# A 7-tap convolution and a two-layer channel mixer in fp32 on one core: the third group's second matmul is taken as seven half products, with the weight sums and several transfers moved

## The chip, the cores and the metric

One core of a Trainium2 chip. The metric is the device time of one execution in microseconds; lower is better. All data is fp32.

## What is computed

```python
# x: (8, 4224, 192); weight: (8 heads, 7 taps); w1: (192, 768); w2: (768, 192)
w = softmax(weight, axis=-1)
y[b, s, h*24 + g] = sum_k w[h, k] * x[b, s - 6 + k, h*24 + g]     # zeros ahead of s = 0
xn = (y - mean(y)) / sqrt(var(y) + 1e-6) * g_ln                   # over the 192 channels
out = y + relu(xn @ w1) @ w2
```

## The kernel before, in words

**Groups.** The rows are cut into NG = 18 groups of 128 partitions by n rows: n is 6, 8 (the rows left over, from all eight sequences), 10, and then 16 for the other fifteen. Group g is one turn of the loop at L973. `groups` (L70) holds them. Group 0, 1 and 2 are the start of the pipeline.

**What a group needs.** `load_x` (L132) brings x with six rows of padding into a tile `xg` (two buffers in turn, so a load waits until the group two before it is done with its x). The convolution is split by taps: tap 0 by `first_tap` on ScalarE (ACT; L369), tap 1 for some groups by `second_tap` (L382), which makes the product on ACT into a tile `tb` and adds it to y by an accumulating DMA on GpSimd's (POOL's) queue, the other taps by `conv` on VectorE (DVE; L397), one instruction for each tap and head (24 channels). `transpose` (L408) makes yt, in 32 by 32 blocks, six chunks of 32 channels. `moments` and `root` (L425, L436) make 1/sqrt(var), which is applied only at the end; the mean is taken out of w1 beforehand.

**The two matmuls.** On TensorE (PE) each fp32 matmul stands in the trace as two records. Groups 0 to 2 do them plainly: `up` (L525) runs six hidden tiles f, each over six chunks c and four blocks q, and `evict_up` (L495) takes each tile out of PSUM with a ReLU on ACT into `ht`, a view of the big tile `room`; `down` (L738) runs six output chunks over six f and four q. From the fourth group on (`fast[g]` not zero; L76, `MIXED` L81), both are Winograd products: matrices in quarters, seven half-size products where the plain form has eight. `up_mixed` (L587) and `down_fast` (L789) do that. They need sums of quarters of w1 and w2 (`w1sums`, `w2sums`, by `sums_of_quarters`, L555), of yt (`sums_of_y`, L569) and of the hidden values (`half_sum`, `lower_sum`, L770 and L777). In `down_fast` the order is: product 1 (a11), product 2 (a21 after `lower_sum`), products 3 and 4; then DVE's `transpose` of the next group, three half sums in place, which may overwrite a12, a11 and a22 only once PE has read them; products 5, 6 and 7 read those. `finish` or `finish_fast` turn the results back into rows; `scale` (ACT) applies the factor and `add_to_out` adds to the output in DRAM by an accumulating DMA on POOL's queue, onto y, which `store_y` (L472) has put there.

**What sets the order.** The whole kernel is in a manual schedule: each engine, and each DMA queue, executes its instructions in the order of the program text, and waits only for data. So the text of the loop L973 to L1027 is the order. In turn g = 0: up(0), conv(1) in two halves of heads with a transpose after each (chunks 0 to 2, then 3 to 5), store of y1, moments, first_tap(2), down(0). In g = 1: conv(2) with six taps, transpose(2), store of y2, first_tap(3), down(1), finish(0), the sums of w2 on DVE, finish(1). In g = 2: conv(3) with six taps, transpose(3), first and second tap of group 4, store of y3 on POOL, down(2), the four sums of w1 on DVE (the last one in place in w1), sums_of_y(3) wholly on DVE, finish(2), moments(3). At its end each of these three groups is parked by ACT copies from PSUM (`park`, L863). Each `load_x(g + 2)` stands at the head of turn g, on SyncE's (SP's) queue. The weights are joined from two words each just before: w1 is complete with the last copy of L360, w2 with L246, L249 and L255 on DVE (`join_words`), called after up(0)'s first tile.

## Time and profile before

| what | value |
|---|---|
| median of 3 runs | 960.58 us (960.49 to 960.9) |
| the profiled execution: its own time | 960.25 us |
| its span, first to last instruction | 958.5 us |
| PE busy | 948.6 us (99%) |
| DVE busy | 895.8 us (93%) |
| ACT busy | 686.6 us (72%) |
| POOL busy | 260.9 us (27%) |
| mean granted TensorE clock | 0.999 of full |
| DMA | 166.69 MB, mean 174 GB/s |

PE's matmuls are pipelined, so its busy share alone doesn't say that it is at its peak. A row of the groups or of the timeline reads: start and length (or busy time), engine, line of the kernel, operation, what it writes and reads, the shapes, how many; in square brackets the idle time of the engine just before and what ended it. A piece of the chain of waits reads: start, length, engine and line, number of instructions. L519 is the matmul of `up` and `up_mixed`, L753 that of `down`, L806 that of `down_fast`.

### The profile page before, as it was taken

The page shows a single profiled execution, that of the slowest core. Times are in us where ns is not written, and L with a number is a line of the kernel's source. Part 1 is how long each engine was busy: PE and PEld are TensorE (multiplying, and loading weights), DVE is VectorE, ACT ScalarE, POOL GpSimd, SP SyncE. Part 2 cuts the span into 40 slices and gives each one's busy share as a digit, 9 for nine tenths or more (in the row PEclk, how much of TensorE's full clock was granted, in tenths as well). Part 3 has the DMA queues.
Part 4 walks back from the last instruction along what each step waited for, and adds up shares of the span by engine and source line. Part 5 has one row for each costly group of instructions (what it writes and reads, how often), then busy time and mean ns, then how long its engine had stood idle before and what let it go on. Part 6 is the DMA issues. An engine that isn't in the chain of part 4 may idle for free.

```text
span 958.5 us, 38499 instructions
## 1 busy us (share of the span) xinstructions
PE 948.6 (99%) x17274; PEld 719.5 (75%) x17274; DVE 895.8 (93%) x1510; ACT 686.6 (72%) x1139; POOL 260.9 (27%) x399
## 2 busy tenths in 40 slices
PE   8999999999999999999999999999999999999997
PEld 7886596776869687786958678686867768586787
DVE  8999998999999999999999999999989999999667
ACT  6625578596877959687796958778695877866461
POOL 1005311612135131422216131341315221161400
PEclk9999999999999999999999999999999999999999
DMA  8243887679697887969788796978879697767241
GB/s 221 79 155 112 180 207 216 146 151 265 134 260 142 235 173 158 249 123 276 136 240 163 178 234 118 281 136 243 158 186 216 120 280 141 179 132 129 53 83 68
DMA packets 28394, 166.69 MB, mean 174 GB/s; under 512 B 3397, under 2 KB 4294, under 8 KB 22215
## 3 DMA queue, kind: packets, MB, share of 16 engines
q0 software_dynamic: 21568, 100.94, 55.0%
q1 hardware_dynamic: 6656, 63.31, 17.9%
q8 instruction: 135, 2.21, 0.9%
q14 instruction: 29, 0.24, 0.1%
q10 hardware_dynamic: 6, 0.00, 0.0%
HBM read 38.93 MB, written 50.33 MB: 93 GB/s over the span
## 4 chain that ended last, share of the span: by engine, by line
PE 97%; ACT 1%; DMA 1%; DVE 0%; SPq 0%; issue 0%; ACTq 0%
PE ps L519 48%; PE ps L806 42%; PE ps L753 6%; DMA xg<-in_x_dram 1%; PE ps L322 1%; ACT w L360 0%; ACT room L618 0%; DVE y L898 0%; ACT spare L241 0%; ACT y L378 0%; PE ps L335 0%; SPq L215 0%; ACT room L509 0%; PE ps L350 0%; SPq L210 0%
## 5 line engine op out<-in xcount | busy, mean ns | idle before, releaser
L403 DVE SCALAR_TENSOR_TENSOR y<-xg,taps,y 128x384 f32<-128x384 f32 (+3 forms) x734 | 367.9, 577 | 1.8 <-issue 1.6
L519 PE MATMUL ps<-yt,w 32*128 32x256 f32 (+2 forms) x4104 | 235.7, 379 | 0.4 <-ACT room L509 0.4
L806 PE MATMUL ps<-room,w2sums 128*32 128x256 f32 (+1 forms) x4320 | 235.9, 375 | 0.0
L618 ACT COPY room<-ps 128x1024 f32<-128x1024 f32 (+1 forms) x135 | 175.0, 1296 | 77.2 <-PE ps L519 76.0
L519 PEld LDWEIGHTS ps<-yt,w 32*128 32x128 f32 x4104 | 204.2, 185 | 26.5 <-issue 9.0
L806 PEld LDWEIGHTS ps<-room,w2sums 128*32 128x32 f32 x4320 | 140.5, 110 | 89.7 <-ACT room L631 4.9
L806 PE MATMUL ps<-room,w 128*32 128x256 f32 (+1 forms) x3240 | 181.0, 375 | 0.4 <-issue 0.4
L773 DVE TENSOR_TENSOR room<-room 128x1024 f32<-128x1024 f32 (+1 forms) x135 | 151.6, 1196 | 21.2 <-PE ps L806 20.0
L806 PEld LDWEIGHTS ps<-room,w 128*32 128x32 f32 x3240 | 104.8, 110 | 68.7 <-DVE room L624 5.0
L519 PE MATMUL ps<-ysums,w1sums 32*128 32x256 f32 x2160 | 124.9, 379 | 0.0
L519 PEld LDWEIGHTS ps<-ysums,w1sums 32*128 32x128 f32 x2160 | 108.7, 185 | 11.2 <-ACT room L618 3.6
L812 ACT COPY cs<-ps 128x256 f32<-128x256 f32 (+1 forms) x180 | 66.0, 369 | 42.6 <-PE ps L806 42.6
L884 ACT ACTIVATE ot<-ot,r 128x192 f32<-128x192 f32 x232 | 93.8, 462 | 0.0
L631 ACT ACTIVATE room<-room 128x1024 f32<-128x1024 f32 (+1 forms) x89 | 92.1, 1071 | 0.0
L891 POOL DMA_DIRECT2D out_dram<-ot x40 | 34.2, 1086 | 194.6 <-ACT ot L884 115.7
L378 ACT ACTIVATE y<-xg,taps 128x384 f32<-128x384 f32 (+3 forms) x141 | 72.8, 611 | 9.0 <-DVE st L434 7.6
L434 DVE BATCH_NORM_STATS2 st<-y 128x6 f32<-128x192 f32 x264 | 70.2, 344 | 0.0
L519 PE MATMUL ps<-yt,w1sums 32*128 32x256 f32 x1080 | 65.1, 379 | 0.0
L812 ACT COPY room<-ps 128x256 f32<-128x256 f32 (+1 forms) x90 | 33.6, 373 | 43.9 <-PE ps L806 42.4
L519 PE MATMUL ps<-ysums,w 32*128 32x256 f32 x1080 | 64.5, 376 | 0.0
L618 ACT ACTIVATE room<-ps 128x1024 f32<-128x1024 f32 (+1 forms) x30 | 43.6, 1454 | 27.6 <-PE ps L519 27.6
L389 ACT ACTIVATE tb<-xg,taps 128x384 f32<-128x384 f32 x112 | 61.9, 635 | 0.0
(109 smaller groups left out, 895.3 us busy)
## 6 DMA issues: line engine op xcount, KB each, us to landing
xg<-in_x_dram SPq DMA_DIRECT2D x15, 2112.0 KB, 19.2
room<-room POOLq DMA_DIRECT2D x45, 512.0 KB, 5.3
out_dram<-ot POOLq DMA_DIRECT2D x29, 768.0 KB, 9.5
y<-tb POOLq DMA_DIRECT2D x28, 768.0 KB, 11.4
out_dram<-y SPq DMA_DIRECT2D x13, 1536.0 KB, 10.8
room<-parts_cs POOLq DMA_DIRECT2D x28, 512.0 KB, 6.6
room<-parts_tb POOLq DMA_DIRECT2D x14, 1024.0 KB, 7.6
xg<-in_x_dram SPq DMA_DIRECT2D x1, 1536.0 KB, 8.0
```

Source lines behind the costliest of these rows:

```text
L378: nc.scalar.mul(y[g][:, 0:n, cs], xg[g][:, 0:n, cs], taps[:, h, 0:1])
L389: nc.scalar.mul(tb[g][:, 0:n, cs], xg[g][:, 1 : 1 + n, cs], taps[:, h, 1:2])
L403: nc.vector.scalar_tensor_tensor(out=y[g][:, 0:n, cs], in0=t[:, k : k + n, cs], scalar=taps[:, h, k : k + 1], in1=y[g][:, 0:n, cs], op0=AL ...
L434: nc.vector.bn_stats(out=sums[g][:, j, :], in_=y[g][:, j, :])
L519: nc.tensor.matmul(banks[:, q, i * w : i * w + w], right[rows, c, P * i : P * i + P], left[rows, :, c, :], start=(first and c == 0 and i = ...
L618: nc.scalar.activation(dst, src, AF.Relu) if relu else nc.scalar.copy(dst, src)
L631: nc.scalar.activation(c, c, AF.Relu)
L753: nc.tensor.matmul(bank[C * q : C * q + C, 0:w], w2[:, f, C * c : C * c + C], left, start=(f == 0), stop=(f == NF - 1),)
L773: nc.vector.tensor_tensor(a[:, *dst, f], a[:, *left, f], a[:, *right, f], op=op)
L806: nc.tensor.matmul(dst[C * q : C * q + C, 0:w], right[:, f, C * c : C * c + C], left[:, f, q], start=(first and f == PAIR), stop=(f == PAI ...
L812: nc.scalar.copy(to[:, c], dst[:, 0:w].rearrange("p (j t) -> p j t", t=t))
L884: nc.scalar.mul(ots[g][:, j, :], ots[g][:, j, :], rstd[g][:, j : j + 1])
```

## The change

Group 2 gets `fast[2] = 10`: its second matmul goes through `down_fast` (seven products of 10 x 16 = 160 columns) instead of `down` (320 columns). `evict_up` writes its hidden tile in the layout of the products, `lower_sum` and `half_sum` run for it on DVE, and `finish_fast(2)` runs in turn 3 instead of `finish(2)` in turn 2. Besides:

- three sums of w1 (128 x 1152) and four of w2 (128 x 288) go from DVE to POOL, and stand behind up(0) in turn 0; the fourth of w1, in place, stays on DVE, in `down_fast(2)` after the transpose;
- the second tap of group 2 and, for six of eight heads, of group 3 goes from DVE's `conv` to ACT and an accumulating DMA (`tb` of group 3 lies in the unused end of `room`);
- the taps of group 3 and 4 on ACT are spread between the hidden tiles (`between`), those of conv(3) over turns 1 and 2, with lower_sum(2) among them;
- moments(1) and root(0) move from turn 1 to turn 0, `sums_of_y(3)` takes POOL for two of its four sums;
- transfers: x of group 3 is issued at the end of conv(1), ahead of the store of y1; x of group 4 on POOL's queue in turn 1 (its padding is zeroed in turn 2); the sixth x (group 5) after `sums_of_y(3)`, behind a small DVE memset; the fourth y (group 3) is stored on POOL's queue in `up_mixed(3)` instead of turn 2.

```diff
@@ -75,6 +75,7 @@
 
     fast = {g: groups[g][2] if g >= 3 else 0 for g in range(NG)}
     fast[NG - 1] = J - 5
+    fast[2] = groups[2][2]
     NFAST = max(fast.values())
     T = C // 2
 
@@ -129,11 +130,13 @@
 
     xg = {}
 
-    def load_x(g, queue=nc.sync):
+    def load_x(g, queue=nc.sync, pad=True, gate=False):
         b, j0, n = groups[g]
         t = xpool.tile([P, J + PAD, D], F32, tag="xg", name=f"xg{g}")
         xg[g] = t
         flat = t.rearrange("p j d -> p (j d)")
+        if gate:
+            nc.vector.memset(t[0:1, 0:1, 0:1], 0.0)
         if b is None:
             for b in range(B):
                 queue.dma_start(
@@ -157,7 +160,8 @@
                     tensor=x.tensor, offset=(b * S - PAD) * D, ap=[[R * D, P], [1, (PAD + n) * D]]
                 ),
             )
-            nc.gpsimd.memset(t[0:1, 0:PAD, :], 0.0)
+            if pad:
+                nc.gpsimd.memset(t[0:1, 0:PAD, :], 0.0)
             return
         nc.gpsimd.memset(t[0:1, 0:PAD, :], 0.0)
         for p0, p1 in ((16, P), (1, 16)):
@@ -382,17 +386,28 @@
     def second_tap(g, heads=(0, H)):
 
         n = groups[g][2]
-        if heads[0] == 0:
+        if heads[0]:
+            pass
+        elif g == 2:
+            part = upool.tile([P, 3 * HJ * CH * C], F32, tag="ys", name="tb2")
+            tb[g] = part[:, 0 : n * D].rearrange("p (j d) -> p j d", d=D)
+        elif g == 3:
+            tb[g] = room[:, (NF * NQ * C - D) * J :].rearrange("p (j d) -> p j d", d=D)
+        else:
             tb[g] = bpool.tile([P, J, D], F32, tag="tb", name=f"tb{g}")
         for h in range(*heads):
             cs = slice(h * GRP, h * GRP + GRP)
             nc.scalar.mul(tb[g][:, 0:n, cs], xg[g][:, 1 : 1 + n, cs], taps[:, h, 1:2])
         if heads[1] == H:
-            for j1, j2 in ((0, n // 2), (n // 2, n)):
-                nc.gpsimd.dma_start(
-                    out=y[g][:, j1:j2].rearrange("p j d -> p (j d)"),
-                    in_=tb[g][:, j1:j2].rearrange("p j d -> p (j d)"), accum_op=ALU.add,
-                )
+            add_second_tap(g)
+
+    def add_second_tap(g, upto=H):
+        n = groups[g][2]
+        for js in (slice(0, n // 2), slice(n // 2, n)):
+            ends = [v[:, js, 0 : upto * GRP] for v in (y[g], tb[g])]
+            if upto == H:
+                ends = [v.rearrange("p j d -> p (j d)") for v in ends]
+            nc.gpsimd.dma_start(out=ends[0], in_=ends[1], accum_op=ALU.add)
 
     def conv(g, k0=1, k1=K, heads=(0, H)):
         n = groups[g][2]
@@ -498,7 +513,7 @@
             dst = ht[g][:, f]
             src = src.rearrange("p q (j t) -> p q j t", t=C)
         elif width(g) == C:
-            dst = ht[g][:, :, f // FC, f % FC].rearrange("p h q j t -> p q h (j t)")
+            dst = of_products(g)[:, :, f // FC, f % FC].rearrange("p h q j t -> p q h (j t)")
             src = src.rearrange("p q (h w) -> p q h w", h=2)
         else:
             dst = ht[g][:, :, f // FC, f % FC].rearrange("p h q j t -> p q j h t")
@@ -522,11 +537,27 @@
                         stop=(last and c == left.shape[2] - 1), skip_group_check=split,
                     )
 
+    def between(g, f):
+
+        if g == 1 and f > 2:
+            second_tap(3, heads=[(0, 2), (2, 5), (5, 6)][f - 3])
+        elif g == 2:
+            if f == 0:
+                scale(0, 0, groups[0][2])
+                add_to_out(0, 0, groups[0][2])
+                nc.gpsimd.memset(xg[4][0:1, 0:PAD, :], 0.0)
+            elif f < 3:
+                m = groups[1][2]
+                scale(1, m * (f - 1) // 2, m * f // 2)
+                if f == 2:
+                    add_to_out(1, 0, m)
+            else:
+                first_tap(4, heads=[(0, 2), (2, 4), (4, 7)][f - 3])
+
     def up(g):
 
 
         n = groups[g][2]
-        scaled = (0, 1) if g == 2 else ()
         hidden_tile(g)
         for f in range(NF):
             banks = take_set()
@@ -537,14 +568,7 @@
                 join_words(w2flat, *words_2)
             if g == 0 and f < 2:
                 first_tap(1, heads=(H // 2 * f, H // 2 * (f + 1)))
-            if 1 <= f <= 4:
-                for s in scaled:
-                    m = groups[s][2]
-                    scale(s, m * (f - 1) // 4, m * f // 4)
-                    if f % 2 == 0:
-                        add_to_out(s, m * (f - 2) // 4, m * f // 4)
-
-
+            between(g, f)
 
     def quarters_of_w1(f0=0, f1=FC):
         return [
@@ -553,9 +577,8 @@
         ]
 
     def sums_of_quarters(dst, b11, b12, b21, b22):
-        d0, d1, d2, d3 = dst
-        for v, a, b in ((d2, b12, b22), (d0, b12, b11), (d1, b22, d0), (d3, b21, d1)):
-            nc.vector.tensor_tensor(v, a, b, op=ALU.subtract)
+        for v, a, b in zip(dst, (b12, b12, b22, b21), (b22, b11, dst[1], dst[2])):
+            nc.gpsimd.tensor_tensor(v, a, b, op=ALU.subtract)
 
     ysums = {}
 
@@ -676,6 +699,8 @@
         else:
             for f in range(PAIR):
                 p.close(p.c11[:, f : f + 1], X, rooms[0][:, f : f + 1], f)
+            if g == 3:
+                store_y(g, nc.gpsimd)
         act_scales(0, 1)
         if last:
 
@@ -819,17 +844,24 @@
         b = quarters_of_w2()
         c11, c21 = cs[:, 0:CH, 0], cs[:, 0:CH, 1]
         c12, c22 = cs[:, CH:NC, 0], cs[:, CH:NC, 1]
-        if g + 2 < NG:
+        if g == 2:
+            work += [lambda h=h: first_tap(4, heads=(h, h + 1)) for h in range(7, H)]
+            work += [lambda h=h: second_tap(4, heads=(h, h + 1)) for h in range(H)]
+        elif g + 2 < NG:
             work += [
                 lambda tap=tap, h=h: tap(g + 2, heads=(h, h + 1))
                 for tap in (first_tap, second_tap) for h in range(H)
             ]
-        product(0, a[:, 0, 0], b[0], c11, True, 3)
-        product(1, a[:, 1, 0], w2sums[:, 2], c22, True, 2)
-        product(1, a[:, 1, 1], w2sums[:, 3], c21, False, 2)
-        product(1, a[:, 0, 1], b[2], None, True, 3)
+        behind = (1, 1, 1, 1) if g == 2 else (3, 2, 2, 3)
+        product(0, a[:, 0, 0], b[0], c11, True, behind[0])
+        product(1, a[:, 1, 0], w2sums[:, 2], c22, True, behind[1])
+        product(1, a[:, 1, 1], w2sums[:, 3], c21, False, behind[2])
+        product(1, a[:, 0, 1], b[2], None, True, behind[3])
         if g + 1 < NG:
             transpose(g + 1)
+            if g == 2:
+                b11, b12 = quarters_of_w1()[0:2]
+                nc.vector.tensor_tensor(b12, b12, b11, op=ALU.subtract)
         half_sum(g, (1, 1), (1, 1), (1, 0), ALU.add)
         half_sum(g, (0, 0), (1, 1), (0, 0), ALU.add)
         half_sum(g, (0, 1), (0, 1), (1, 1), ALU.subtract)
@@ -845,6 +877,8 @@
         product(0, a[:, 0, 1], b[3], c12, False)
         if g + 1 < NG:
             sums_of_y(g + 1, nc.gpsimd)
+            if g == 2:
+                load_x(5, gate=True)
             moments(g + 1)
         else:
             finish_fast(g, 0, flat, cs, parts)
@@ -972,49 +1006,53 @@
 
     for g in range(NG):
         mixed, last = g in MIXED, g + 1 == NG
-        if g + 2 < NG:
+        if g + 2 < NG and g not in (1, 2, 3):
             load_x(g + 2)
         if mixed:
             work = up_mixed(g, ahead(g), pending)
             pending = iter(())
         else:
             up(g)
-        if not fast[g]:
-
-            if g:
-                conv(g + 1)
-                transpose(g + 1)
-            else:
-                early = CH * C // GRP
-                conv(1, heads=(0, early))
-                transpose(1, 0, CH)
-                conv(1, heads=(early, H))
-                transpose(1, CH, NC)
-            if g < 2:
-                store_y(g + 1)
-                moments(g)
-            first_tap(g + 2)
-            if g == 2:
-
-                second_tap(g + 2)
-                store_y(g + 1, nc.gpsimd)
+            work = []
+        if g == 0:
+            w11, w12, w21, w22 = quarters_of_w1()
+            for v, a, b in zip((1, 0, 2), (w12, w11, w21), (w22, w1sums[:, 1], w1sums[:, 0])):
+                nc.gpsimd.tensor_tensor(w1sums[:, v], a, b, op=ALU.subtract)
+            sums_of_quarters([w2sums[:, v] for v in (2, 0, 1, 3)], *quarters_of_w2())
+            early = CH * C // GRP
+            conv(1, heads=(0, early))
+            transpose(1, 0, CH)
+            conv(1, heads=(early, H))
+            transpose(1, CH, NC)
+            load_x(3)
+            store_y(1)
+            moments(0)
+            moments(1)
+            first_tap(2)
+            second_tap(2)
+            next(root(0, True))
+        elif g == 1:
+            conv(2, 2)
+            transpose(2)
+            store_y(2)
+            first_tap(3)
+            add_second_tap(3, 6)
+            load_x(4, nc.gpsimd, pad=False)
+        elif g == 2:
+            conv(3, 2, 5, heads=(0, 6))
+            lower_sum(2)
+            conv(3, 5, K, heads=(0, 6))
+        if g < 2:
             down(g)
             park(g)
             if g == 1:
+                moments(2)
                 finish(0)
-                next(root(0, True))
-                sums_of_quarters([w2sums[:, v] for v in range(4)], *quarters_of_w2())
-                moments(2)
                 next(root(2, True))
+                conv(3, heads=(6, H))
                 finish(1)
-            elif g == 2:
-                b11, b12, b21, b22 = quarters_of_w1()
-                sums_of_quarters([b12] + [w1sums[:, v] for v in range(3)], b11, b12, b21, b22)
-                sums_of_y(3, nc.vector)
-                finish(2)
-                moments(3)
             continue
-        if g + 2 < NG:
+        if g > 2 and g + 2 < NG:
             store_y(g + 1)
         results = down_fast(g, work)
         if last:
```

## The prediction

> **What bounds the kernel now.** I read the chain of waits first, in order of time, then the waits of TensorE (PE), then the timelines of VectorE (DVE) and GpSimd (POOL) in the first 125 us. Pieces of the chain (start, length, what):
>
> ```profile
> 31.00 6.25 PE ps L519 x144
> 37.25 11.84 PE ps L753 x288
> 49.09 15.75 PE ps L519 x288
> 64.84 15.68 PE ps L753 x288
> 80.52 19.59 PE ps L519 x288
> 100.11 19.52 PE ps L753 x288
> 943.60 8.19 PE ps L753 x240
> ```
>
> From 31.00 us each piece is PE and starts where the last one ended: the span is a sum of matmuls, and the third group's second matmul (g = 2) is the 19.52 us at 100.11. PE's only waits of 0.9 us or more are before 15 us. So a saved matmul is a saved time, and any wait put before a matmul is a lost time. What stands ready just in time is DVE's work:
>
> ```profile
> 27.09 1.36 DVE L246 SCALAR_TENSOR_TENSOR spare<-raw,spare 128x1152 f32<-128x1152 uint32 x1 [1.40 <-ACT spare L229]
> 28.91 1.36 DVE L249 SCALAR_TENSOR_TENSOR spare<-raw,spare 128x1152 uint32<-128x1152 uint32 x1 [0.47 <-ACT spare L241]
> 30.30 1.36 DVE L255 TENSOR_TENSOR w<-spare 128x1152 f32<-128x1152 f32 x1
> 31.58 7.98 DVE L403 SCALAR_TENSOR_TENSOR y<-xg,taps,y 128x192 f32<-128x192 f32 x24
> 39.60 0.98 DVE L414 STREAM_TRANSPOSE yt<-y 128x768 f32<-128x768 f32 x1
> 40.50 7.96 DVE L403 SCALAR_TENSOR_TENSOR y<-xg,taps,y 128x192 f32<-128x192 f32 x24
> 48.49 0.98 DVE L414 STREAM_TRANSPOSE yt<-y 128x768 f32<-128x768 f32 x1
> ```
>
> The last of these ends at 49.47. It makes chunks 3 to 5 of yt for up(1), which begins at 49.09 and reaches chunk 3 after half of its first hidden tile (15.75 / 6 / 2 = 1.31 us), at 50.40. **The slack is 0.93 us**, the smallest near the change. Also, w2 is ready at 31.66 and wanted at 37.25.
>
> **What the Trainium skill says.** (1) "SBUF — State Buffer", section "Who interferes with whom": a DVE instruction with two SBUF inputs contends with a GpSimd instruction that reads SBUF, the lock is held for the whole instruction, and the second to come is blocked. The trace agrees from GpSimd's side: its tiny operations double once DVE runs two-input convolution steps beside them.
>
> ```profile
> 77.26 0.21 POOL L464 TENSOR_TENSOR d<-r 128x14 f32<-128x14 f32 x1
> 81.33 0.20 POOL L464 TENSOR_TENSOR d<-r 128x10 f32<-128x10 f32 x1
> 83.18 0.45 POOL L464 TENSOR_TENSOR d<-r 128x10 f32<-128x10 f32 x1
> ```
>
> Every one of them from 81.61 on gets in at the next DVE boundary. The reverse is hinted at once: the DVE step of L230 that starts at 4.68, beside a GpSimd select of 128 elements, took 0.47 us and its two sisters 0.35. A long GpSimd sum beside a two-input DVE step occurs nowhere in this trace: the long ones (L581, L582) lie beside moments, which have one input. (2) "GPSIMD Engine Reference", section 3.1: a two-input sum costs about 2.6 cycles of 1.2 GHz per element, the two reads sharing one port. The trace agrees:
>
> ```profile
> 172.38 1.83 POOL L581 TENSOR_TENSOR ysums<-yt 128x768 f32<-128x768 f32 x1 [4.83 <-PE ps L806]
> ```
>
> (1.83 - 0.21) / (768 - 14) = 2.15 ns per element.
>
> **The change, part by part.**
>
> **Seven products.** Removed: 288 records, 19.52 us. Added: 7 x 3 x 3 x 4 = 252 matmuls, 504 records, of 10 x 16 = 160 columns. The last group's L753 has just that shape: 8.19 us / 240 = 34.1 ns. 504 x 34.1 = 17.2 us. **Gain 2.3 us**, all on the path. That the shorter products don't pay is excluded by this row.
>
> **The sums on GpSimd.** Three of 1152 elements (A): 0.2 + 1152 x 2.15 ns = 2.66 us each; four of 288 (B): 0.80 us each. Only set-up work that ends at 5.7 us precedes them on POOL's queue, and the A's wait only for the last copy of w1 (L360, ends 26.00), so they start at 26.1, beside DVE's L246 to L255; the B's wait for w2 and start beside conv(1), all two-input steps. What DVE loses to one is not shown. Upper bound: the whole 2.66 and 0.80; lower bound: the two reads at one per cycle, from the page, 1.92 and 0.48; below that, nothing, is a rival. I take the streaming part, 2.48 and 0.62. With turns at each boundary: A1 holds L246 from 27.09 to 28.7; A2 runs from its end at 30.05 to 32.5; L249 to 33.85; A3 to 36.3; L255 to 37.7 instead of 31.66. Slip 6.0 us (the 1.4 and 0.5 us of idle before are used up). Four B's add 4 x 0.62 = 2.5. **DVE slips 8.5 us** (6.4 to 9.4), down(0) starts 0.4 us late because of w2, and up(1) stops at chunk 3 for the rest: **PE loses 8.5 - 0.93 = 7.6 us** (5.5 to 8.5).
>
> **DVE's new order up to the half sums**, with the times it would have without that slip: 14 moments to 52.97; conv(2) with five taps instead of six, 40 x 0.383 (18.39 / 48) to 68.3; transpose 2.1, 10 moments 2.6, finish(0) 1.6 to 74.6; two heads of conv(3), 12 x 0.533, to 81.0; finish(1) 2.0; 18 steps of conv(3), 9.6, to 92.6; lower_sum, 3 x 0.744 (the 704-element rows, 7.30 / 9 = 0.811, less 64 elements at 1.04 ns) to 94.8; 12 steps to 101.2; transpose 3.3; one w1 sum 1.36, to **105.9**. PE ends the third product at 100.11 + 3 x 72 x 0.0341 = **107.5**; only then may the half sum overwrite its input. Slack 1.6 us, and 0.7 with both slips (8.5 and 7.6). From there three half sums (2.23 us) stand against one product (2.46 us): slack 0.2, as in the last group (2.43 against 2.7), which ran through. Cost nothing; if this cover is gone, one for one. The removed second matmul's copies (6, ACT) and DVE's other three w1 sums and w2 sums were off the path: nothing.
>
> **ACT.** second_tap(2), 8 x 0.40 us, follows first_tap(2) to 44.4 and holds up three parking copies, whose banks PE wants at 49.09: nothing. second_tap(3) and first_tap(4) fill gaps of 1.6 and 2.0 us between evictions, in pieces of 1.0 to 1.6 us; PE has two sets of banks, so one tile's time covers it.
>
> **Accumulating DMAs of the second taps.** Group 2's is issued at 44.4, behind the sums; the transfers are idle there, and landings of 7 to 12.4 us (the median here) give 51 to 57, against conv(2) at 53.0, or 61.5 with the slip: nothing with it, up to 2.4 us without. Group 3's has rows of 576 bytes, 2,048 instead of 256 pieces, which no row shows: 10 to 14 us from about 72, so 82 to 86 against conv(3) at 83.0: up to 3 us late, of which 1.6 (or 0.7) is covered. I take nothing and keep 2 us for the range.
>
> **Moved transfers.** The third x is issued ahead of the first y's eight stores on SP's queue, at the end of conv(1), and lands some 9.7 us later, before second_tap(3) in up(1)'s fourth tile. The fourth x goes to POOL's queue behind group 3's accumulation; its memset then holds POOL until it has landed, with only stores of group 1's outputs behind it: ACT's first_tap(4) starts 13 us into up(2), so nothing. The fifth x waits for DVE's memset at about 117 and is wanted at 156 (first_tap(5)): nothing. The third y's store, behind the first adds of up_mixed(3) on POOL, lands by about 146 (18.2 us here), before y5 takes its buffer at 156: nothing. In group 3, finish_fast costs DVE some 3.9 us where finish took 2.47; its wait of 1.46 us (L624, 143.5) covers it.
>
> **Sum.** Profiled time 960.25 (span 958.5 and 1.75 around it): - 2.3 + 7.6 = 965.6. The median of the runs is 0.33 above the profiled one: **965.9**.
>
> **Rivals.** *No hindrance (faster).* If DVE's steps run beside a GpSimd sum as they do beside GpSimd's tiny ones (0.53 us apart at 83 us as at 90), DVE slips nothing, the 0.93 us holds and the 2.3 us stays: 958.3. The point of decision is a DVE slip of 0.93 + 2.3 = 3.2 us: below it the kernel is faster, above it slower. For it: only GpSimd's waiting is plain in the trace. Against: those tiny operations read 10 elements in a step's pause, and the 0.47 us of L230. *Partly: no hindrance, but a later wait.* Group 2's or 3's accumulation lands late, or the half sums miss their 0.2 us: 1 to 4 us returned, 959 to 962. *Both:* full hindrance (8.5) and group 3's accumulation 2 to 4 us late: 968 to 971, and more if generating 2,048 pieces is slow.
>
> **How the numbers follow.** Hindrance as worked out 0.65 (963.5 to 967.5); no hindrance 0.18; partly 0.08; both 0.09. About 0.2% (1.9 us) is what a measurement of this kernel can tell from no change: below 958.7 counts as faster, above 962.5 as slower. Faster 0.18 + 0.01 = 0.19; same 0.06; slower 0.75. The forecast and its costlier neighbour hold 0.74, so the range has to reach to the faster case: 957.9 to 970; the likeliest case's own range is 963.5 to 967.5.
>
> **What would show it.** In the profile after: L753 down(2) gone and 504 records of L806 in about 17.2 us; POOL sums of some 2.7 us from 26 us on, and DVE's L246, L249, L255 stretched or started late, w2 ready near 37.7; PE waiting some 7 us for DVE's transposed y (L414) near 50 us in up(1); no wait between there and the half sums. The prediction is wrong if DVE's conv(1) keeps its 0.33 us step with the sums beside it, or if PE's wait comes in the third group instead.

## The result, and the profile after

| | before | after |
|---|---|---|
| median | 960.58 us (960.49 to 962.14, 5 runs) | 970.65 us (970.27 to 971.06, 5 runs) |
| profiled execution; its span | 960.25; 958.5 us | 971.06; 969.1 us |

The ratio is 1.0101 (95% interval 1.0087 to 1.0116): the change costs 10.1 us, nearly twice the 5.3 us of the forecast.

PE's stages, each from its first matmul to the next stage's first, show where. The rows left out agree within 0.1 us.

| stage of PE | before, us | after, us | difference |
|---|---|---|---|
| start of up(0), and up(0) | 37.18 | 36.83 | -0.35 |
| up(1) | 15.75 | 25.18 | **+9.43** |
| second matmul of group 2 | 19.52 | 17.66 | -1.86 |
| up_mixed(3) | 27.82 | 29.30 | +1.48 |
| down_fast(9) and down_fast(10) | 54.88 | 55.57 | +0.69 |
| up_mixed(12) | 27.96 | 30.04 | +2.08 |
| down_fast(12) | 28.39 | 27.44 | -0.95 |

They add up to +10.5. The chain of waits of the kernel after (start, length, what), where the one of before had PE alone, with up(1) at 49.09:

```profile
36.60 10.20 DVE y L418 x24
46.83 0.98 DVE yt L429
47.81 7.88 DVE y L418 x24
55.71 0.99 DVE yt L429
56.75 17.16 PE ps L534 x264
73.91 15.68 PE ps L778 x288
89.59 19.64 PE ps L534 x288
```

The chain leaves PE for VectorE up to 56.75: PE stands still in up(1) until the second transpose of conv(1) is there. Of its waits in the first 160 us (in total, times, longest), those that are new:

```profile
PE ps L534 <- DVE yt L429: 6.5, 1, 6.5
PE ps L534 <- issue: 0.8, 1, 0.8
PE ps L778 <- DVE w L259: 0.5, 1, 0.5
PE ps L831 <- ACT cs L837: 0.2, 1, 0.2
```

The first line is the wait that the prediction named. The timeline of VectorE shows what made it late, and that of GpSimd what lay beside:

```profile
26.12 3.16 DVE L250 SCALAR_TENSOR_TENSOR spare<-raw,spare 128x1152 f32<-128x1152 uint32 x1 [0.56 <-ACT spare L233]
29.20 3.78 DVE L253 SCALAR_TENSOR_TENSOR spare<-raw,spare 128x1152 uint32<-128x1152 uint32 x1
33.02 3.67 DVE L259 TENSOR_TENSOR w<-spare 128x1152 f32<-128x1152 f32 x1
36.60 10.19 DVE L418 SCALAR_TENSOR_TENSOR y<-xg,taps,y 128x192 f32<-128x192 f32 x24
47.73 7.95 DVE L418 SCALAR_TENSOR_TENSOR y<-xg,taps,y 128x192 f32<-128x192 f32 x24
```

```profile
25.11 2.95 POOL L1020 TENSOR_TENSOR w1sums<-w 128x1152 f32<-128x1152 f32 x1 [19.41 <-ACT w L364]
28.14 7.33 POOL L1020 TENSOR_TENSOR w1sums<-w,w1sums 128x1152 f32<-128x1152 f32 x2
36.76 1.79 POOL L581 TENSOR_TENSOR w2sums<-w 128x288 f32<-128x288 f32 x2 [1.30 <-DVE w L259]
38.63 1.69 POOL L581 TENSOR_TENSOR w2sums<-w,w2sums 128x288 f32<-128x288 f32 x2
```

The three joining steps took 1.36 us each before and take 3.2 to 3.8 beside the w1 sums; the 24 convolution steps beside the w2 sums take 10.19 us for 7.98, and the next 24, with no sum beside, 7.95 again. Instruction by instruction, the two engines take turns: the joining steps end at 29.27, 32.98 and 36.68, each 1.2 us after a w1 sum (28.06, 31.77, 35.46), and just four convolution steps are long, 0.96 us for 0.41, each ending 0.2 us after a w2 sum. The last transpose ends at 56.69 instead of 49.47.

But 6.5 us of waiting are not 9.4. The rest shows in the windows of the two kernels (stretch, its length, PE busy and its instructions, weight loads, DVE, ACT, POOL, then the granted clock of PE, DMA share, GB/s). After, with the stretch behind the stop and the next one:

```profile
56.50:62.10 5.60, 5.35 (x52) 4.46 (x56) 5.60 (x20) 1.02 (x1) 1.53 (x5) 0.50 1.02 350
62.10:73.84 11.74, 11.74 (x220) 10.32 (x212) 11.74 (x32) 6.52 (x9) 4.33 (x15) 1.00 0.25 87
```

Before, the same stretch:

```profile
56.50:62.10 5.60, 5.60 (x112) 5.32 (x108) 5.60 (x16) 2.05 (x2) 0.00 (x0) 1.00 0.71 296
```

PE is granted half its clock (52 matmuls instead of 112) from 55.3 to 62.1 us, 6.83 us. The 264 matmuls left of up(1) take 17.16 us; at full clock they are 15.75 x 264 / 288 = 14.44. So up(1) loses some 6.7 us to the stop and **2.7 us to the clock behind it**.

### The profile page after: what moved, and what is told of

Same layout as the page of the kernel before. It is cut to its first block, busy times and chain, and to the rows that moved or that the text cites. A ratio compares the mean times of both kernels' runs of the same rounds, so it can differ in the third digit from the quotient of the medians.

```text
span 969.1 us, 38983 instructions
## 1 busy us (share of the span) xinstructions
PE 950.8 (98%) x17490; PEld 730.7 (75%) x17490; DVE 901.4 (93%) x1506; ACT 695.3 (72%) x1165; POOL 289.3 (30%) x412
## 3 DMA queue, kind: packets, MB, share of 16 engines
q0 software_dynamic: 23936, 105.26, 56.9%
## 4 chain that ended last, share of the span: by engine, by line
PE 91%; DVE 3%; DMA 2%; ACT 1%; POOL 1%; issue 1%; SPq 0%; DVEq 0%; POOLq 0%; ACTq 0%
PE ps L534 45%; PE ps L831 43%; PE ps L778 2%; DVE y L418 2%; DMA xg<-in_x_dram 1%; PE ps L369 1%; ACT room L641 0%; DMA room<-room 0%; DVE spare L253 0%; DVE spare L250 0%; SPq L142 0%; ACT y L382 0%; DVE yt L429 0%; POOL d L461 0%; POOL room L608 0%
## 5 line engine op out<-in xcount | busy, mean ns | idle before, releaser
L418 DVE SCALAR_TENSOR_TENSOR y<-xg,taps,y 128x384 f32<-128x384 f32 (+3 forms) x720 | 363.9, 582 | 2.2 <-DMA y<-room 1.6
L831 PE MATMUL ps<-room,w2sums 128*32 128x256 f32 (+2 forms) x4608 | 246.5, 370 | 0.2 <-ACT cs L837 0.2
L831 PEld LDWEIGHTS ps<-room,w2sums 128*32 128x32 f32 x4608 | 149.2, 110 | 91.5 <-ACT room L654 5.3
L831 PE MATMUL ps<-room,w 128*32 128x256 f32 (+2 forms) x3456 | 188.6, 370 | 0.1
L798 DVE TENSOR_TENSOR room<-room 128x1024 f32<-128x1024 f32 (+2 forms) x147 | 160.6, 1165 | 23.0 <-PE ps L831 21.1
L831 PEld LDWEIGHTS ps<-room,w 128*32 128x32 f32 x3456 | 112.4, 110 | 68.1 <-DVE room L647 5.0
L534 PEld LDWEIGHTS ps<-ysums,w1sums 32*128 32x128 f32 x2160 | 109.4, 185 | 11.8 <-issue 3.7
L837 ACT COPY cs<-ps 128x256 f32<-128x256 f32 (+2 forms) x192 | 69.8, 366 | 44.2 <-PE ps L831 44.1
L837 ACT COPY room<-ps 128x256 f32<-128x256 f32 (+2 forms) x96 | 35.3, 367 | 48.3 <-PE ps L831 46.4
L400 ACT ACTIVATE tb<-xg,taps 128x384 f32<-128x384 f32 (+1 forms) x120 | 66.0, 626 | 0.0
L410 POOL DMA_DIRECT2D y<-tb x30 | 26.6, 1048 | 122.6 <-ACT room L837 109.5
```

The costliest lines, as they stand in the source:

```text
L400: nc.scalar.mul(tb[g][:, 0:n, cs], xg[g][:, 1 : 1 + n, cs], taps[:, h, 1:2])
L418: nc.vector.scalar_tensor_tensor(out=y[g][:, 0:n, cs], in0=t[:, k : k + n, cs], scalar=taps[:, h, k : k + 1], in1=y[g][:, 0:n, cs], op0=AL ...
L534: nc.tensor.matmul(banks[:, q, i * w : i * w + w], right[rows, c, P * i : P * i + P], left[rows, :, c, :], start=(first and c == 0 and i = ...
L798: nc.vector.tensor_tensor(a[:, *dst, f], a[:, *left, f], a[:, *right, f], op=op)
L831: nc.tensor.matmul(dst[C * q : C * q + C, 0:w], right[:, f, C * c : C * c + C], left[:, f, q], start=(first and f == PAIR), stop=(f == PAI ...
L837: nc.scalar.copy(to[:, c], dst[:, 0:w].rearrange("p (j t) -> p j t", t=t))
```

## The experiments

The theory from these two profiles: GpSimd's sums hold up VectorE's two-input steps, PE stops in up(1), and the stop brings a half clock; the rest of the loss (+1.5 us in up_mixed(3), +2.1 us in up_mixed(12)) comes from elsewhere. The rivals stand with the runs. The kernel before, run beside each set, gave medians of 960.45 to 961.29 us.

### Is it the sums, and is it their reading?

**a1_memsets**: the sums become memsets of the same tiles.

```diff
-                nc.gpsimd.tensor_tensor(w1sums[:, v], a, b, op=ALU.subtract)
+                nc.gpsimd.memset(w1sums[:, v], 0.0)
-            nc.gpsimd.tensor_tensor(v, a, b, op=ALU.subtract)
+            nc.gpsimd.memset(v, 0.0)
```

> The changed kernel with GpSimd's seven sums of w1 and w2 replaced by memsets of the same tiles (the sums are left out, so the output isn't the reference's; every other instruction stays). Theory A, the sums block VectorE [...]: memsets read nothing, so L246's and conv(1)'s counterparts keep 1.36 and 0.33 us, TensorE's wait of 6.5 us and the 0.5 us for w2 go, and with them the half clock (2.7 us): about 961 (970.65 - 9.7). Theory B, GpSimd being busy at all, or the transfers moved around conv(1), make VectorE late: the wait stays and the time is 969 to 971.

Measured: 964.05 us, ratio 1.0032 (1.0023 to 1.004). up(1) is 15.75 us at full clock; up_mixed(3) keeps 29.29 and up_mixed(12) 30.03. So without the sums the stop and the half clock behind it are gone. Whether it is their reading, the run doesn't tell as it was meant to: a memset waits for no weights, so the seven ran at 5.6 to 11.1 us, long before the joining steps and conv(1), and met other steps of VectorE:

```profile
5.64 3.67 POOL L1020 MEMSET w1sums<- 128x1152 f32 x3
9.27 1.80 POOL L581 MEMSET w2sums<- 128x288 f32 x4
```

```profile
5.83 1.29 DVE L234 TENSOR_SCALAR room<-room 128x384 uint32<-128x384 uint32 x1
7.15 1.18 DVE L238 TENSOR_SCALAR room<-room 128x384 int32<-128x384 int32 x1
8.24 1.29 DVE L232 TENSOR_SCALAR room<-room 128x384 uint32<-128x384 uint32 x1
...
10.43 0.54 DVE L250 SCALAR_TENSOR_TENSOR room<-room 128x384 f32<-128x384 uint32 x1
10.89 0.54 DVE L253 SCALAR_TENSOR_TENSOR room<-room 128x384 uint32<-128x384 uint32 x1
```

The first three have one input and take 1.2 to 1.3 us, where the kernel after has 0.34 to 0.36; each ends 0.2 us after a memset. The last two have two inputs and take what they take there (0.55). So a write alone does hold up some one-input steps, and that it lets two-input steps pass rests on these two short ones. The held steps lie on this run's chain of waits: the start and up(0) take 39.3 us instead of 36.8, which is most of the 3 us over the expectation.

**b1_sums_early**: the kernel before with only the sums (three of w1, four of w2) given to GpSimd behind up(0).

```diff
...
-            nc.vector.tensor_tensor(v, a, b, op=ALU.subtract)
+            nc.gpsimd.tensor_tensor(v, a, b, op=ALU.subtract)
...
             else:
+                w11, w12, w21, w22 = quarters_of_w1()
+                for v, a, b in zip((1, 0, 2), (w12, w11, w21), (w22, w1sums[:, 1], w1sums[:, 0])):
+                    nc.gpsimd.tensor_tensor(w1sums[:, v], a, b, op=ALU.subtract)
+                sums_of_quarters([w2sums[:, v] for v in range(4)], *quarters_of_w2())
                 early = CH * C // GRP
```

> The kernel before with one part of the change alone: three sums of w1 and four of w2 on GpSimd behind up(0), the fourth of w1 on VectorE where it was. Theory A: the stop in up(1) comes back by itself, 0.4 us for w2, some 6.5 us for the transposed y and 2.7 us at half clock: 969.5 to 970.5. Theory B (the moved transfers or the other moved steps cause it): within 1 us of the kernel before, 960 to 961.

Measured: 970.08 us, ratio 1.0094 (1.007 to 1.0119). PE's waits in that kernel from 25 to 165 us:

```profile
PE ps L519 <- DVE yt L414: 6.5, 1, 6.5
PE ps L753 <- DVE w L255: 0.2, 1, 0.2
```

The same 6.5 us, and a half clock of 10.24 us. This one part, alone, costs as much as the whole change.

### Is the rest of up(1) the clock?

**e1_w2_alone**: only the three w1 sums become memsets.

```diff
-                nc.gpsimd.tensor_tensor(w1sums[:, v], a, b, op=ALU.subtract)
+                nc.gpsimd.memset(w1sums[:, v], 0.0)
```

> The kernel after with GpSimd's four sums of w2 kept and its three of w1 replaced by memsets of the same tiles, so the products that use them multiply by zeros (left out: the values of the three w1 sums). Dose test for PE's wait in up(1). By the steps measured, the w2 sums delay VectorE by 4 x 0.55 = 2.2 us, less the slack of 0.9 us: PE waits 1.3 us. Theory H (the half clock comes from the length of the stop): a stop this short leaves the clock at 1.0, so up(1) is 15.75 + 1.3 = 17 us and not 17 + 2.7. Rival (any stop of PE here brings the half clock): up(1) 19 to 20 us. Time for H: 970.65 - 9.4 + 1.3 = 962.5; rival 965.

Measured: 965.12 us, ratio 1.004 (1.0028 to 1.0052). up(1) is 17.12 us, as theory H has it, and the clock stays at 1.0. VectorE's timeline in this run shows the dose of the w2 sums alone:

```profile
29.60 1.36 DVE L253 SCALAR_TENSOR_TENSOR spare<-raw,spare 128x1152 uint32<-128x1152 uint32 x1 [0.52 <-ACT spare L245]
30.99 1.36 DVE L259 TENSOR_TENSOR w<-spare 128x1152 f32<-128x1152 f32 x1
32.27 10.17 DVE L418 SCALAR_TENSOR_TENSOR y<-xg,taps,y 128x192 f32<-128x192 f32 x24
43.37 7.95 DVE L418 SCALAR_TENSOR_TENSOR y<-xg,taps,y 128x192 f32<-128x192 f32 x24
```

2.2 us for four sums, 0.55 each, and the joining steps are free again. The time is 2.6 us over the expectation, that of the profiled run (964.06 us, the fastest) 1.6: PE had a gap of 1.4 us in down_fast(8), and the start and up(0) took 1.1 us more than in the kernel after, with the memsets beside one-input steps as in a1.

**a2_busy_wait**: in up(1), 24 matmuls into an idle bank while PE would wait.

```diff
...
+                for _ in range(24):
+                    nc.tensor.matmul(
+                        idle[:, 0:P], w1[:, 0, 0:P], w1[:, 0, 0:P], start=True, stop=True
+                    )
```

> The changed kernel with 24 matmuls of 128x128x128 into an unused PSUM bank between chunks 2 and 3 of up(1)'s first tile, some 6 us of work, so that TensorE isn't idle in its wait. Theory A with the clock as a consequence of the idle time: the granted clock stays at 1.0 from 56 to 62 us and the time falls by the 2.7 us that half clock costs, to about 968. Rival: the slow matmuls after the wait have another cause (transfers of x and y at that time): no change, 970.5, or more if the extra matmuls end after VectorE.

Measured: 971.41 us, ratio 1.011 (1.0082 to 1.0138). up(1) fell to 22.54 us with the clock at 1.0: the 2.6 us of the clock came back as expected. The total did not fall, since up_mixed(12) took 32.97 us in this profile, with a half clock of its own at 651 us. So the stage confirms the theory, the total doesn't.

### Sums that don't read beside two-input steps

**c1_act_dma_sums**: the sums as negations on ACT, then accumulating DMAs (`weight_sums`, called in three steps).

```diff
-            sums_of_quarters([w2sums[:, v] for v in (2, 0, 1, 3)], *quarters_of_w2())
+            second_tap(2)
+            weight_sums(0)
...
+        if g == 1 and f == 1:
+            weight_sums(1)
```

> The changed kernel with the seven sums made without VectorE and GpSimd reading: ScalarE writes the negated subtrahend (7 steps, some 5.5 us, in its idle stretches of turns 0 and 1) and an accumulating DMA adds the other quarter. Theory A: up(1) takes 15.75 us again and the clock stays up; what is left of the change is the shorter second matmul (-1.9) against the 1.5 us in up_mixed(3) and the 2 us in turn 12: 960 to 962. If the added DMAs make the second tap of group 2 or 3 late, VectorE's slack of 1.6 us before the half sums goes and TensorE waits there instead: up to 964.

Measured: 970.84 us, ratio 1.0112 (1.0095 to 1.013). VectorE was free (1.36 us a joining step) and yt ready at 48.4, yet the second step made ACT, in order, wait for an accumulating DMA ahead of an eviction of up(1), and PE waited 8.7 us for that. A miss of the edit: it exchanged one late engine for another.

**d1_beside_moments**: the sums on GpSimd again, each set held by a one-element memset of VectorE until VectorE begins moments, which have one input.

```diff
+            nc.vector.memset(w2sums[0:1, 2, 0:1, 0:1], 0.0)
             load_x(3)
...
             second_tap(2)
+            sums_of_quarters([w2sums[:, v] for v in (2, 0, 1, 3)], *quarters_of_w2())
...
             load_x(4, nc.gpsimd, pad=False)
+            for v, a, b in zip((1, 0, 2), (w12, w11, w21), (w22, w1sums[:, 1], w1sums[:, 0])):
+                nc.gpsimd.tensor_tensor(w1sums[:, v], a, b, op=ALU.subtract)
```

> The kernel after, with GpSimd's seven sums moved to the stretches in which VectorE works on one input only: the w2 sums behind the second tap of group 2, held by a one-element write of VectorE until it begins the moments (51.6 to 55.3 us in the run with memsets), the w1 sums behind the x4 load, held until VectorE begins the moments of group 2 and the transposes of finish(0) (73.9 to 78.1 us). Theory A (a sum delays VectorE only while VectorE runs operations with two inputs): the convolution steps of group 1 stay at 0.33 us, the wait in up(1) and the half clock vanish (15.75 us instead of 25.18), the third w1 sum overlaps the convolution of group 3 and costs VectorE 2 to 4 us that its waits of 1.6 and 2.0 us take up: down_fast(2) 17.7 to 19. Rival (GpSimd's work as such is what delays, wherever it stands): the 8 us only move, to up(2) or down_fast(2). Theory C, the fetch of PE's instructions, keeps the 1.5 us in up_mixed(3), and the stop of GpSimd's queue the 2.1 us in the turn of group 12. Sum for A: 960.5 - 1.85 + 1.5 + 2.1 = 962.2; with up to 1.3 us more in down_fast(2), 963.5. The rival: 968 or more.

Measured: 968.43 us, ratio 1.0071 (1.0059 to 1.0083). Theory A held for the w2 sums: up(1) 15.75 us, the 13 moments beside them unchanged. The w1 sums came later than I had put them (71.8 to 81.6 us) and met conv(3): in VectorE's timeline of this run

```profile
72.67 1.66 DVE L957 STREAM_TRANSPOSE ot<-parked 128x192 f32<-128x192 f32 x6
74.25 12.57 DVE L418 SCALAR_TENSOR_TENSOR y<-xg,taps,y 128x384 f32<-128x384 f32 x12
```

The twelve steps take 6.4 us in the runs without a sum beside. The slack that I had counted on wasn't enough: PE waited 3.8 us for the half sums in down_fast(2) (109.70 to 113.84), then had a gap of 2.4 us for instructions (118.64 to 121.08), and 3.41 us of half clock from 122.0. So the rival's "it only moves" is what the misplaced w1 sums did, and the total is the rival's too (968 or more); it is up(1) and the moments that tell the two apart.

### The gap in up_mixed(3)

PE's gap of 0.8 us "for issue" (1.16 us between matmuls, 129.81 to 130.97) waits for nothing that the profile shows. The DMA queue "instruction" moves one packet of 16 KB for every 256 of PE's records (137 packets, 34,980 records), and the packet of that stretch went from 128.66 to 129.60, beside the load of x5 issued at 126.1. Theory C: PE ran out of instructions because that fetch was late.

**a3_x5**: x5 is loaded at the head of turn 3, some 16 us earlier.

```diff
-        if g + 2 < NG and g not in (1, 2, 3):
+        if g + 2 < NG and g not in (1, 2):
...
-            if g == 2:
-                load_x(5, gate=True)
```

> The changed kernel with the sixth x loaded at the head of turn 3, as before the change, and without the memset that held it: its load is then issued some 16 us earlier, when its buffer is free (about 110 us), not at 126 us. Theory C: the 1.5 us that up_mixed(3) lost in the profile (a gap of 0.8 us in TensorE that no semaphore ends, and 0.6 us beside it) come from TensorE's instructions being fetched beside this 2.1 MB transfer: 969.2. Rival: the gap has to do with the GpSimd sums of yt or with chance: 970.6 and the gap at the same place, or none in either.

Measured: 973.81 us, ratio 1.014 (1.0108 to 1.0172). up_mixed(3) is 27.90 us, but down_fast(2) now has a gap of 2.2 us (124.91 to 127.09), its packet at 124.88. The gap didn't go, it came one block of 256 records earlier. (The profiled run, 972.19 us, is the fastest of the four; what the others lose isn't shown.) **c2_x5_later** (c1, with x5 behind `finish_fast(2)` in turn 3) only halved the gap, to 0.63 us:

> The same, and the sixth x loaded behind finish_fast(2), some 8 us later than in the changed kernel, when TensorE's block of instructions for up_mixed(3) has been fetched. Theory C: the gap of 1.2 us in up_mixed(3) goes (29.3 to 27.9 us for that stage) and comes nowhere else, and the time is 1.4 us under the kernel it is built on: 958.5 to 960.5. Rival: the fetch is late whatever x does: no difference between the two.

Measured: 971.75 us, ratio 1.0111 (1.0097 to 1.0125); up_mixed(3) 30.01 us, with a new gap of 0.58 us for data at 152.9. With x5 moved, the gap moves or shrinks, and neither run is faster for it.

The packets of all the kept profiles say more. Behind the start they have 19 such gaps of over 0.15 us, and in every one PE goes on at a boundary of 256 records, 1.3 to 1.5 us after a packet has landed: PE does run out of instructions. And the blocks in question are those of the seven products. They are used up in 4.2 to 4.8 us each, where a block of down(2) lasted 8.6 us and most others last 6.9. The packet of the next block starts up to 4.8 us after PE has entered a block there, and takes about 1 us, so it can come too late for the short blocks. Fourteen of the fifteen kernels with the seven products have a gap at one of the two boundaries around the end of down_fast(2), b2 below too, which moves no transfer (1.65 us, 122.79 to 124.44), and the fifteenth, e1, loses 0.5 us in up_mixed(3); the kernel before and b1, with down(2), have none there. So the gap comes with the seven products. Why a packet starts at once in one run and over 4 us later in another isn't shown.

### The 2.1 us in the turn of group 12

GpSimd issues its first accumulating DMA of up_mixed(12) 1.9 us late, after an idle time that nothing explains, and PE waits 1.5 us for ACT in the end.

**a4_pool_shift**: 24 tiny memsets ahead on GpSimd, to see whether a count of instructions sets the place.

```diff
+    for _ in range(24):
+        nc.gpsimd.memset(shift, 0.0)
```

> The changed kernel with 24 one-element memsets on GpSimd added among its first instructions (under 6 us, in a stretch where it is idle). In turn 12 GpSimd starts its first accumulating DMA 1.9 us late, always at the same instruction and with no wait that the profile shows, and TensorE loses 2.1 us by it. Theory D: GpSimd stands there for its own instructions, at a fixed count; with 24 more in front the stop falls elsewhere and turn 12's up_mixed takes 27.96 us instead of 30.04: 968.5. Rival: the stop belongs to the time (about 630 to 650 us) or to that DMA: no change, 970.6.

Measured: 974.02 us, ratio 1.0131 (1.0117 to 1.0145). The stop stayed at the same DMA (up_mixed(12) 29.67 us): that theory falls. (The time is 3.4 us over the kernel after because the chain of waits at the start runs through the added memsets: 42.0 us for the start and up(0) instead of 36.8.) Counting packets of GpSimd's queue (q0) instead, the late issue lies in every profile, a4's too, where they come to 16,190 to 16,370: at 633 us in the kernel after, at 521 and 527 us in c1 (with more DMAs on that queue), at 709.8 us in the kernel before, on a store that nobody waits for. Two runs add one idle DMA of 512 elements early on that queue:

```diff
...
+                nc.gpsimd.dma_start(out=shift[:, 8:16:2], in_=shift[:, 0:8:2])
```

**a5_more_packets** is the kernel after with it, **d2_more_packets** is d1 with it.

> The kernel after with the same idle DMA of 512 elements alone, the sums where the change put them. Theory Q: up(1) stays at 25.2 us and up_mixed(3) at 29.3, the turn of group 12 falls from 30.04 to 27.96 us: 968.5 to 969, ratio to before 1.008. Rival: the stop stays at the accumulating DMA of that turn and the time at 970.6.

> The run above with one more DMA of GpSimd's queue in the second turn, 512 elements of 4 bytes in a tile of its own, which nothing uses. Theory Q: in every profile so far one issue on GpSimd's DMA queue comes 0.9 to 1.9 us late where the queue's packets reach some 16,200 to 16,400 (2 to the 14 is 16,384); in the kernel before this falls on a store that nobody waits for, at 709.8 us, and in the kernel after on the accumulating DMA at 633.5 us, which PE waits for in the end. 512 packets more put it some 20 us earlier, on a store at about 612 us: the turn of group 12 then takes 27.96 us instead of 30.04, and the time is 2.1 us less than the run above, 960 to 961.5. Rival (the stop belongs to that DMA or that turn): it stays in the same place, and the time is unchanged within 0.3 us.

Measured: a5 968.82 us, ratio 1.0082 (1.0066 to 1.0097); d2 966.63 us, ratio 1.0057 (1.0044 to 1.007). In both, up_mixed(12) takes 27.96 us and PE waits for nothing there. (The profile of a5 is of its slowest run, 972.08 us; only its stages are read here.) The same stage takes 27.96 to 28.14 us in all five runs with the idle DMA, and 29.67 to 32.97 in all seven with the packets of the kernel after. GpSimd's timeline in the kernel after, at that place:

```profile
628.63 1.05 POOL L164 MEMSET xg<- 1x1152 f32 x1
633.52 0.88 POOL L608 DMA_DIRECT2D room<-room  x1 [3.85 <-ACT room L641]
```

and in a5, where the late issue is the store at 610.31, with an idle time 1.2 us longer than in other turns:

```profile
610.31 0.87 POOL L927 DMA_DIRECT2D out_dram<-ot  x1 [9.34 <-ACT cs L839]
...
634.68 0.88 POOL L610 DMA_DIRECT2D room<-room  x1 [1.94 <-ACT room L643]
```

The idle time ahead of the accumulating DMA is 1.94 us again instead of 3.85. Theory Q stands, with one correction: the trace has the idle DMA's 512 elements in only 32 packets, and the late store comes at packet 15,760, so what counts is the pieces (15,760 - 32 + 512 = 16,240, the count of the kernel before). The change, with 23,936 packets on that queue instead of 21,568, moved the stop from a store to a DMA on PE's path. Why the queue stops there isn't shown.

### Could the seven products stand alone?

**b2_seven_alone**: the kernel before with `fast[2] = groups[2][2]` and what it needs, nothing moved.

```diff
+    fast[2] = groups[2][2]
...
-            down(g)
-            park(g)
+            if g == 2:
+                results = down_fast(g, [])
+            else:
+                down(g)
+                park(g)
```

> The kernel before with the seven products for the third group alone: the weight sums, the taps and the transfers stay where they were, lower_sum(2) stands between the fourth and fifth tap of conv(3), the transpose and the half sums in the second matmul. The second matmul has 1.9 us less of work, but VectorE reaches the first half sum only at about 112.5 us, 5 us after TensorE has read its input, and the sums of w1 and yt come 2 to 3 us late for up_mixed(3); if the waits are long enough for half clock another 2 to 3 us: 965 to 969. Rival (VectorE has the room): 958.5 to 960.

Measured: 974.78 us, ratio 1.0143 (1.0128 to 1.0158), 5.8 us over the upper end of the expectation. down_fast(2) took 27.25 us and up_mixed(3) 32.02. PE waited 5.2 us for ACT's copies of the products, and ACT had been busy from 101.2 to 109.4 us with sixteen taps of group 4, which stand ahead of the copies in its order; and 4.1 us for an addition of VectorE (L625, at the end of up_mixed(3)), with half clocks behind both. So the edit has a flaw of its own, the place of these taps. That VectorE has no room for the half sums where it stands is worked out, not seen by itself: its transpose ended at 112.4, and PE, without its stop, would have read the third product's input by 107.3.

### All sums beside one-input work

**d3_four_windows** spreads the sums over four stretches with d2's idle DMA; **d4_sum_before_tap** mends the one that came late in it; **d5_windows_again** places them once more. The core of d5 against the kernel after (`one_sum` is one subtraction on GpSimd):

```diff
+            nc.vector.memset(w2sums[0:1, 2, 0:1, 0:1], 0.0)    # ahead of moments(0)
+                one_sum(w2sums, v)                             # all four, behind second_tap(2)
+            nc.vector.memset(w1sums[0:1, 1, 0:1, 0:1], 0.0)    # ahead of transpose(2)
+            one_sum(w1sums, 1)
+                nc.vector.memset(w1sums[0:1, 0, 0:1, 0:1], 0.0)  # ahead of finish(1)
+                one_sum(w1sums, 0)
+            nc.vector.memset(w1sums[0:1, 2, 0:1, 0:1], 0.0)    # ahead of transpose(3)
+            one_sum(w1sums, 2)
```

> The kernel after, with the seven sums of GpSimd spread over four stretches in which VectorE works on one input, each held by a one-element write of VectorE (one w1 and one w2 sum beside the moments of groups 0 and 1, one w1 sum beside the moments of group 2, three w2 sums beside the transposes of finish(1), the last w1 sum beside transpose(3)), and with the idle DMA of 512 elements that moves the stop of GpSimd's queue. Theory A: up(1) 15.75 us at full clock, down_fast(2) 17.7 to 18.5 us, the turn of group 12 27.96 us; up_mixed(3) keeps the fetch gap at 29.1 to 29.5 us. Sum: 960.6 - 1.85 + 1.5 + 0.3 = 960.5, that is no more than the kernel before within 0.2%: the fetch gap takes the gain back. Rival F (the gap belongs to the disturbed order and goes with it): up_mixed(3) 27.9 us and 958.8. Rival S (sums delay VectorE also beside one-input work): down_fast(2) or up(1) over 20 us, 964 or more.

> The run with four windows, with the last w1 sum issued ahead of the second tap's DMA on GpSimd, so that it runs beside transpose(3) at 103.5 to 106.2 us. Theory A: the half sums take 6.7 us again, PE's wait of 4.2 us in down_fast(2) and the half clock of 3.4 us go, down_fast(2) is 17.7 to 18.0 us instead of 24.37. If up_mixed(3) keeps the 27.90 us of that run: 965.3 - 6.6 = 958.7, 0.2% less than the kernel before; if the fetch gap returns (theory C, since group 2 again comes at the pace of the kernel after): up_mixed(3) 29.3 us and 960.1, no difference from before. Rival S (a sum delays VectorE also beside the transpose): transpose(3) over 4.5 us, down_fast(2) 19 us or more, 961.5 or more.

> The run before with the sums placed anew: all four w2 sums beside the moments of groups 0 and 1, one w1 sum beside transpose(2) and the moments of group 2, one beside the transposes of finish(1), one beside transpose(3). VectorE's delay ahead of transpose(3) falls from 3.0 to some 0.7 us, the half sums are in time, and PE doesn't wait for them. If the late fetch in down_fast(2) follows from PE's short stop: no gap there, down_fast(2) 17.7 us and not 23.23, no half clock, and the time 963.2 - 5.5 = 957.7 if up_mixed(3) stays at 27.90 us, or 959.2 if the gap of the kernel after comes back there (29.3). Rival (the late fetch belongs to the place, whatever PE does): down_fast(2) 22 us or more, and 962 to 963.

| run | median, us | ratio (interval) | down_fast(2), us | up_mixed(3), us |
|---|---|---|---|---|
| d3 | 965.31 | 1.0044 (1.0029 to 1.0059) | 24.37 | 27.90 |
| d4 | 963.20 | 1.0018 (1.0007 to 1.0028) | 23.23 | 27.90 |
| d5 | 961.28 | 1.0004 (0.9995 to 1.0012) | 20.43 | 28.10 |

All three missed their expectations, by 4.8, 3.1 and 2.1 us at the least. All three have up(1) at 15.75 us and up_mixed(12) at 27.96 to 28.14. In d3 the last w1 sum was queued behind GpSimd's DMAs and met the half sums (10.2 us for 6.7), and PE waited 4.2 us. In d4 PE waited only 0.7 us for them, but then 2.85 us for instructions, with a half clock behind. In d5 that sum runs at full pace beside the transpose: on VectorE

```profile
103.23 0.06 DVE L866 MEMSET w1sums<- 1x1 f32 x1
103.39 3.38 DVE L431 STREAM_TRANSPOSE yt<-y 128x3072 f32<-128x3072 f32 x1
```

and on GpSimd

```profile
103.46 2.67 POOL L591 TENSOR_TENSOR w1sums<-w,w1sums 128x1152 f32<-128x1152 f32 x1 [4.13 <-DVE w1sums L866]
```

Both take what they take alone (3.38 and the 2.66 us worked out before). Another w1 sum of d5 missed its place: it began when the transposes of finish(1) were over, and one step of conv(3) took 2.97 us instead of 0.60, which the slack ahead of the half sums covered.

```profile
82.70 2.62 POOL L591 TENSOR_TENSOR w1sums<-w,w1sums 128x1152 f32<-128x1152 f32 x1
```

```profile
82.77 7.73 DVE L420 SCALAR_TENSOR_TENSOR y<-xg,taps,y 128x384 f32<-128x384 f32 x10
```

What d5 has left is in its chain of waits:

```profile
110.27 5.09 PE ps L841 x142
115.36 1.91 issue
117.28 2.88 PE ps L841 x73
120.15 28.10 PE ps L536 x501
```

1.91 us "issue" (2.2 us between matmuls), again behind a late instruction packet, takes back what the seven products gain. I had expected it to go with PE's short stop; it stayed, so the rival of that run is nearer (2.2 us against 2.85 in d4, though with no half clock). Here x5 is issued only after the gap, so x5 can't be what delays this fetch. With no sum that makes PE wait, and with the idle DMA, the change is as fast as the kernel before, not faster.

## Why the prediction was right in direction and wrong in size

- **Seven products, gain 2.3 us: nearly.** The stage gains 1.86 us; 0.2 us is a wait for ACT's copies, which come late behind the pieces of first_tap(4), and the records take some 34.6 ns for 34.1.
- **The sums delay VectorE by 8.5 us: right in kind and near in size.** The last transpose is 7.2 us late, and the turns that the prediction worked out stand in the trace. The Trainium skill's "SBUF — State Buffer", section "Who interferes with whom", has a VectorE instruction with two SBUF inputs contend with a GpSimd instruction that reads SBUF, and the runs agree: b1 shows the loss alone, and the w2 sums of d1 beside moments and the last sum of d5 beside a transpose cost nothing. The rival "no hindrance" is dead. One hint was misread: L230, with its 0.47 us at 4.68, has one input, so it speaks for the kind of hold that the memsets of a1 show, not for this one.
- **The first step that failed is the one from VectorE's slip to PE's loss**, "PE loses 8.5 - 0.93 = 7.6 us": it priced a stop at its length. PE stopped for some 6.7 us, but the clock was half for 6.83 us, and the matmuls behind the stop cost 2.7 us more: 9.4 us. The Trainium skill's "TensorE: Matmul & The Clock Gate", Part 1, "What's actually happening", says that the clock falls to half after an idle window and rises after a busy one, in windows of 3413 ns that run freely. The runs agree: every half-clock stretch is 3.41, 6.83 or 10.24 us, but for those at the kernels' very end. They also show that length alone doesn't decide (lengths are from matmul to matmul): 1.5 us (e1) left the clock alone, and so did the 4.1 us of d1, which by the later edges lay half in each of two windows (2.1 us in either), while the 2.4 us behind it fell into one window (118.6 to 122.0) and brought the half clock. In d2 a stop of the same 4.1 us (109.65 to 113.78) covered a whole window (110.3 to 113.7) and brought it too. a2 kept PE busy and had those 2.6 us back in the stage.
- **The second step that failed, and the larger part of the miss, is what was put at nothing**: 3.6 us. Of it, 2.1 us is the stop of GpSimd's queue, which the moved second taps and x4, with their packets on that queue, put in PE's way, under "Moved transfers". The other 1.5 us is the late fetch of instructions, and it belongs to the seven products ("all on the path"): their gain was taken from the length of the records alone, and they use up a block of instructions in half the time. Neither is on a row that I read as a resource. No accumulation came late to VectorE by enough to reach PE.
- The half sums' slack held: no stop there in the kernel after.

The sum as it came: - 1.9 + 6.7 + 2.7 + 1.5 + 2.1, and - 0.6 of small gaps and the start, is + 10.5, for the forecast's - 2.3 + 7.6.

**Open**: why a packet of PE's instructions starts late at some places and not at others; why GpSimd's queue stops at that count; what a write on GpSimd does to longer two-input steps.

## What to carry to other kernels

Work given to an idle engine must be placed beside what it doesn't disturb: a GpSimd sum cost VectorE most of its own duration beside two-input steps and nothing beside transposes and moments. A one-element write is enough to hold it until then, but not to make it start then: behind other work in GpSimd's order it can still come late, as in d1, d3 and d5. Price a stop of the matmul engine at its length, and from some 2.4 us on allow for a half clock behind it, which cost 2.7 us here. When every stage runs at the bound, a gain of 2 us has to be held against things that no engine's row shows, such as where a queue's stop will fall, or whether shorter instructions are used up faster than they are fetched.

## What the runs showed of the hardware that I had not expected

- PE's instructions come in packets of 16 KB by a DMA queue of their own, one per 256 records. A block late for its turn stops PE by 0.5 to 2.9 us, shown as "issue" (a3, d3, d4, d5), and PE goes on 1.3 to 1.5 us after the packet has landed. Short records make it likelier: 4.2 to 4.8 us a block here for 8.6. The kernel before has one such gap too (0.7 us in down_fast(12)), which the kernel after doesn't.
- GpSimd's DMA queue is late by 0.7 to 1.9 us at about 16,200 to 16,400 pieces; 512 pieces more moved the stop to an earlier store and gave back 2 us.
- A gap of 2.4 us that filled 70% of one clock window halved the clock, one of 4.1 us across two windows didn't (d1), and one of 4.1 us over a whole window did (d2).
- Transposes and moments of VectorE beside a GpSimd sum lose nothing, and neither does the sum: 3.38 and 2.67 us (d5). But one-input TENSOR_SCALAR steps beside a GpSimd memset took 1.2 to 1.3 us for 0.35 (a1).
